# Batch 0's squares and the embeddings later at the start, transfers booked at 400 GB/s, and first turned tiles asked earlier in the second mixture

## The chip, the cores and the metric

The kernel runs on one core of one Trainium2 chip. The metric is device microseconds (us) of one execution. The engines are TensorE (PE; its weight loads are PEld), VectorE (DVE), ScalarE (ACT), GpSimd (POOL) and SyncE (SP), which here issues almost all transfers.

## The reference

Three layers follow each other. The sizes are x (8, 8, 512, 64), state (8, 8, 32, 64), 4608 tokens of 512 numbers, 2048 hidden units, and 8 experts with 1024 hidden units each.

```python
scores = scale * x @ state.T;  a = exp(scores - max);  a /= a.sum + 1e-9
xread = a @ state                                  # every x row reads the state
a2 = softmax(scale * state @ x.T) ; sread = a2 @ x # every state row reads x
tok = concat([xread, sread], axis=2) -> (4608, 512)
h = tok @ w_in ; r = max(h, 0) ; y = (r * r) @ w_out             # 512 -> 2048 -> 512
logits = unit(y) @ unit(expert_emb).T / tau ; e = argmax(logits)
gate = softmax(logits)[e]
out = gate * (max(y @ w1[e], 0) @ w2[e])                         # 512 -> 1024 -> 512
```

## The kernel before

All work is put in order by a greedy planner, the class `Plan`, when the program is built. Each piece of work is a generator, a thread with a priority, that yields an engine with an estimated cost (`yield act(1260)`), an event (`yield ev("st", 0)`), or a pool of buffers. `run` picks the step that can start first by these costs, and of equal ones the smaller priority; the order in which it picks them is the order in which the instructions of each engine stand, and that order is fixed on the chip. Transfers have a booked time too:

```python
self.dma_free = max(self.dma_free, self.cur[2]) + nbytes / 350e3   # Plan.dma: bytes per us
return self.dma_free + 2.0
phl_slots.release(t + LATE)       # weights of the experts: a buffer is free LATE us after the booked store
```

The figures move nothing on the chip by themselves: they say when the planner takes a transfer to be there, and so in which order it puts the work.

Products are split into two halves of FP16 each, three matmuls for one (lines 1442 to 1444 of the first up-projection, 1527 to 1529 of its down-projection, 1840 to 1842 and 1881 of the experts'). Each part needs a scale, a power of two from the sum of squares (`pow2`), so squares are taken all through the kernel.

**The start.** SP loads state and x of batch 0 and then the 16 blocks of w_in and w_out, 1 MB each, into buffers that are used for other things later (`RAW_IN`, names such as g, stage, wo_t, he). Each block is converted by ACT and DVE (L916, L929, L931), and for w_in a bound on the columns is found: products with itself on TensorE (L962), a diagonal of that on DVE (L971), its squares on ACT (L976), sums over partitions (L985) and a maximum on DVE (L991). From two blocks' maxima comes the scale `swi` of w_in (L999 to L303). Batch 0 goes through at once (`first_attention`, `first_scores`, `first_scale`): its x is used in FP32, its attention is applied to the product of state and w_in (S, then sw, L678), and `first_scale` squares x (L623, two operations of ACT) for the scale `sx` of batch 0. `embeddings` squares and scales the experts' embeddings on DVE (the reciprocal root `rsqrt` is lines 309 to 315). It runs at once when its small loads are there.

**Batches.** Batches 1 to 7 follow in order, and the state side of batch 0, which is called batch "B" there, stands between batches 2 and 3 (`ATT`). `late_side` waits for x of batch 0 and asks for its state side, whose two exponentials are L780 (he, rt with the factor `eighth`). x lies in the buffer xx; when the late side gives it back (`xf_slots.release()`), the other layout of x can be loaded.

**The first mixture and routing.** The up-projections u (L1442) with relu and square on ACT and DVE (L1395, L1409, L1414), and the down-projections d (L1527; in FP32 at L1505 for the first tokens) run over the batches. Each tile of 128 tokens becomes a record `rec`; a DMA transpose of it (xr, L1279, asked by SP) feeds the router's matmuls t (L1289), and POOL scatters the record to DRAM (L1368).

**The second mixture.** Tokens are sorted into tiles of one expert each. For a tile, POOL gathers its records (`gather`, L1766, name rec2), SP asks for a DMA transpose, the turn (`turn`, L1786, name xes), and `fetch_weights` loads the expert's w1 and w2 where they are not there already (L1744, 2 MB each; buffers stage and xx hold w1, he and sw hold w2). All these loads and turns stand in SP's one queue in a fixed order. In `fetch`, the loads of tile 0 wait for `ev("experts")` and `ev("attention")`, those of tile 1 also for

```python
if t == 1:
    yield ev("moe1") if name == "w2" else ev("cum", NXT - 1)
    yield ev("xe", 0)          # the first turn, as booked to be done
```

Of the kernel before, what the change touches and what calls it, by code (L numbers as in the profile page):

```python
# [10 lines left out]
F32 = mybir.dt.float32  # L11
# [52 lines left out]
PRIO_E1 = 2.2  # L64
PRIO_SW = 1.27
TINY = 0.18
LATE = 3.0


C_ID = 0  # L70
# [34 lines left out]
class Plan:  # L105
# [32 lines left out]

    def dma(self, nbytes):

        self.dma_free = max(self.dma_free, self.cur[2]) + nbytes / 350e3
        return self.dma_free + 2.0

    def _advance(self, th):
# [102 lines left out]
def moe_kernel(  # L247
# [317 lines left out]
    def first_attention():  # L565

        yield ev("st", 0)
        stt = st_t.pop(0)
        yield xhl_slots
        xh, xl = halves_tile()  # L570
        ss = small.tile([128, 3], F32, name="ss")
        yield act(490)
        nc.scalar.activation(out=xl.bitcast(BF16)[:, :, :64], in_=stt, func=AF.Square, accum_out=ss[:, 2:3])
        yield t_slots
        p = ps_t.tile([128, 512], F32, name="t")
        yield "pe", 0.2
        mm(p[:, 2:3], lhsT=one32, rhs=ss[:, 2:3], start=True, stop=True)
        mm(p[:, 256:512], lhsT=oneb, rhs=xl.bitcast(BF16)[:, :, :64], start=True, stop=True)
        for t in range(2):
            plan.add(first_scores(t, xh, xl, stt), 0.4 + 0.1 * t)  # L580
        plan.add(first_scale(ss, stt), 0.95)
        v = small.tile([128, 2], F32, name="sv")[:, 0:1]
        yield tiny(4)
        V.tensor_scalar(out=v, in0=p[:, 2:3], scalar1=FLOOR, scalar2=None, op0=ALU.max)
        pow2(sx[:, 1:2], isx[:, 1:2], v, 204)
        yield sth_slots
        sthl = att.tile([128, 2, 4, 64], F16, name="sthl")
        stf = sthl.rearrange("p a c n -> p (a c n)").bitcast(F32).rearrange("p (c n) -> p c n", c=4)
        yield dve2(256)
        V.tensor_scalar(out=stf, in0=stt, scalar1=sx[:, 1:2], scalar2=float(2.0 ** -14), op0=ALU.mult, op1=ALU.mult)  # L590
        ev("stf").set()
        plan.add(first_state_w(stf), 0.6)
        plan.add(group_bound(0, p), 0.7)
# [15 lines left out]
        yield from weigher(0, Sp.rearrange("p a (h n) -> p (a h) n", n=NS), xh, xl, eighth, 16 * t, 16 * t + 16,  # L609
                           lambda: u_slots.release(k_h))  # L610

    def first_scale(ss, stt):

        for t in range(2):
            yield ev("scored", t)
        yield ev("stf")
        st_slots.release()
        xf = xf_t.pop((0, 0))
        for i in range(2):
            yield pjk_slots  # L620
            jk = att.tile([128, 2, 512], BF16, name="pjk")
            yield act(1260)
            nc.scalar.activation(out=jk, in_=xf[:, 2 * i:2 * i + 2], func=AF.Square, accum_out=ss[:, i:i + 1])  # L623
            pjk_slots.release()
        xf_slots.release()
        at = plan.now()
        yield t_slots
        plan.cur[2] = max(at, plan.now())
# [11 lines left out]
    def late_side():  # L640

        yield ev("x", B, 0)
        yield ev("st", B)
        xf, stt = xf_t.pop((B, 0)), st_t.pop(B)
        yield ev("att", ATT[ATT.index(B) - 1])
        plan.add(state_side(B, ((stt, xf),), eighth), PRIO_S0)
        for C in range(2):
            yield ev("ST", B, C)
        xf_slots.release()
        st_slots.release()  # L650

# [99 lines left out]
    def state_side(b, pairs, scl):  # L751
# [37 lines left out]
        nc.sync.dma_start_transpose(e, eb[:, 1024:2048].bitcast(F16))  # L789
        turned = plan.dma(1 << 19) + 1.0  # L790
        yield ev("x", b, 1)
        xs = xf_t.pop((b, 1))
        yield xhl_slots
        xsh, xsl = halves_tile()
# [425 lines left out]
    def embeddings():  # L1220
# [3 lines left out]
        nc.scalar.dma_start(cs16, cst16)  # L1224
        plan.cur[2] += 2.5
        ev("identb").set()
        yield tiny(3)
        V.reciprocal(out=itau, in_=tsb)
        V.tensor_scalar(out=itau, in0=itau, scalar1=float(2.0 ** -14), scalar2=None, op0=ALU.mult)
# [484 lines left out]
    def fetch_weights(t0, t1):  # L1714
        def fetch(name, done, ts, slots, src):
            last = None
            for t in ts:
# [9 lines left out]
                else:  # L1727
# [4 lines left out]
                    if t == 1:  # L1732

                        yield ev("moe1") if name == "w2" else ev("cum", NXT - 1)
                        yield ev("xe", 0)
                sides = sides_of(t)
                for i, a in enumerate(sides):
                    if i and last + 1 < t:
# [17 lines left out]
    def gather(t0, t1, m2):  # L1756
        for t in range(t0, t1):
# [1 line left out]
            yield ev("idx", which)  # L1759
            yield ev("records", (NT if which else SEEN) - 1)  # L1760
            if t == 2:
                yield ev("xe", 0)
            yield rec2_slots
            r = m2.tile([128, REC], F32, name="rec2", bufs=6)
            yield "pool", 1.1
# [14 lines left out]
    def turn(t0, t1, m2):  # L1780
        for t in range(t0, t1):
# [2 lines left out]
            xe = m2.tile([128, 8, 128], F16, name="xes", bufs=XE)  # L1784
            yield "sp", 0.06
            nc.sync.dma_start_transpose(xe, rec_t[t].bitcast(F16)[:, 0:1024])  # L1786
            plan.cur[2] = plan.dma(1 << 18) + 1.0
            xe_t[t] = xe
            ev("xe", t).set()
# [220 lines left out]
```

## Time and profile before

| | us |
|---|---|
| three runs | 1068.17, 1074.14, 1078.63 |
| their median | 1074.14 |
| the profiled execution, its own time | 1067.83 |
| span of its trace | 1066.0 |
| TensorE busy in it | 1029.7 (97%) |
| VectorE busy | 671.4 (63%) |
| ScalarE busy | 591.9 (56%) |
| GpSimd busy | 125.8 (12%) |
| moved by DMA | 212.93 MB, 200 GB/s on average |

The time of an execution holds the span and 1.8 us around it. All times of the trace count from the start of the span, in one profiled execution. The busy shares are averages over stages with different limits.

### The profile page before, as it was taken

The page shows a single profiled execution, that of the slowest core. Times are in us where ns is not written, and L with a number is a line of the kernel's source. Part 1 is how long each engine was busy: PE and PEld are TensorE (multiplying, and loading weights), DVE is VectorE, ACT ScalarE, POOL GpSimd, SP SyncE. Part 2 cuts the span into 40 slices and gives each one's busy share as a digit, 9 for nine tenths or more (in the row PEclk, how much of TensorE's full clock was granted, in tenths as well). Part 3 has the DMA queues.
Part 4 walks back from the last instruction along what each step waited for, and adds up shares of the span by engine and source line. Part 5 has one row for each costly group of instructions (what it writes and reads, how often), then busy time and mean ns, then how long its engine had stood idle before and what let it go on. Part 6 is the DMA issues. An engine that isn't in the chain of part 4 may idle for free. (4 is left out here: it accounts for less than half of the span.)

```text
span 1066.0 us, 26360 instructions
## 1 busy us (share of the span) xinstructions
PE 1029.7 (97%) x10631; PEld 670.7 (63%) x10631; DVE 671.4 (63%) x1835; ACT 591.9 (56%) x986; POOL 125.8 (12%) x149
## 2 busy tenths in 40 slices
PE   5899999999999999989999999899999999999998
PEld 4555555565655565546655667577767677767675
DVE  6899898689797888877877876356322223222222
ACT  5999987788888798777887895110111011111110
POOL 0000001002002010020020010312112121212111
PEclk9999999999999999999999999999999999999999
DMA  8943656827757568676575896954894677684692
GB/s 302 342 146 112 170 163 143 269 75 167 245 115 223 163 184 240 170 188 195 129 225 156 238 327 222 287 136 110 277 317 108 206 236 228 190 257 114 214 324 80
DMA packets 161600, 212.93 MB, mean 200 GB/s; under 512 B 112257, under 2 KB 115201, under 8 KB 156098
## 3 DMA queue, kind: packets, MB, share of 16 engines
q1 hardware_dynamic: 152722, 184.04, 59.6%
q0 software_dynamic: 8320, 27.08, 7.8%
q8 instruction: 85, 1.39, 0.5%
q14 instruction: 41, 0.34, 0.1%
q10 hardware_dynamic: 432, 0.08, 0.0%
HBM read 259.10 MB, written 51.68 MB: 292 GB/s over the span
## 5 line engine op out<-in xcount | busy, mean ns | idle before, releaser
L1796 ACT ACTIVATE r<-u 128x512 f32<-128x512 f32 x70 | 41.8, 597 | 321.4 <-PE u L1842 304.0
L1527 PE MATMUL d<-wo_t,g 128*128 128x512 f16 x512 | 194.1, 379 | 0.9 <-DVE rec L318 0.9
L1529 PE MATMUL d<-wo_t,g 128*128 128x512 f16 x512 | 194.1, 379 | 0.6 <-DVE g L1414 0.6
L1528 PE MATMUL d<-wo_t,g 128*128 128x512 f16 x512 | 194.0, 379 | 0.0
L1442 PE MATMUL u<-aT,sw 128*128 128x256 f16 x512 | 140.8, 275 | 4.0 <-ACT r L1395 3.4
L1444 PE MATMUL u<-aT,sw 128*128 128x256 f16 x512 | 140.5, 274 | 0.0
L1443 PE MATMUL u<-aT,sw 128*128 128x256 f16 x512 | 140.5, 274 | 0.0
L1799 DVE CAST hh<-r 128x512 f16<-128x512 f32 x70 | 29.9, 427 | 156.5 <-ACT r L1796 155.0
L1395 ACT ACTIVATE r<-u,cg 128x512 f32<-128x512 f32 x128 | 87.5, 684 | 55.3 <-PE u L1444 42.1
L1368 POOL DMA_INDIRECT rec_d<-rec,pi x34 | 39.5, 1163 | 471.7 <-ACT r L1409 178.0
L1414 DVE TENSOR_TENSOR g<-r,g 128x512 f16<-128x512 f32 x128 | 87.1, 687 | 4.8 <-ACT r L1409 3.4
L1529 PEld LDWEIGHTS <-g 128*128 128x128 f16 x512 | 50.1, 98 | 61.8 <-DVE g L1414 1.6
L1810 DVE TENSOR_SCALAR o<-d,rec,wo_t 128x512 f32<-128x512 f32 x35 | 28.3, 809 | 83.9 <-PE d L1881 80.9
L1528 PEld LDWEIGHTS <-g 128*128 128x128 f16 x512 | 50.1, 98 | 48.0 <-issue 1.1
L1409 ACT ACTIVATE r<-r 128x512 f32<-128x512 f32 x128 | 79.4, 627 | 1.4
L1527 PEld LDWEIGHTS <-g 128*128 128x128 f16 x512 | 50.2, 98 | 47.5 <-DVE l L1323 0.4
L1881 PEld LDWEIGHTS <-hh 128*128 128x128 f16 (+1 forms) x688 | 50.9, 102 | 43.6 <-issue 0.4
L1840 PE MATMUL u<-xes,stage 128*128 128x128 f16 x448 | 76.0, 219 | 0.8 <-DMA xes<-rec 0.8
L1842 PE MATMUL u<-xes,stage 128*128 128x128 f16 x448 | 76.0, 219 | 0.0
L1841 PE MATMUL u<-xes,stage 128*128 128x128 f16 x448 | 76.0, 219 | 0.0
L1840 PE MATMUL u<-xes,xx 128*128 128x128 f16 x416 | 71.7, 221 | 2.0 <-DMA xx<-w_d 2.0
L1842 PE MATMUL u<-xes,xx 128*128 128x128 f16 x416 | 71.7, 221 | 0.0
(337 smaller groups left out, 2562.7 us busy)
## 6 DMA issues: line engine op xcount, KB each, us to landing
w_d<-he SPq DMA_DIRECT2D x128, 256.0 KB
g<-w_d SPq DMA_DIRECT2D x16, 2048.0 KB
wo_t<-w_d SPq DMA_DIRECT2D x16, 2048.0 KB
stage<-w_d SPq DMA_DIRECT2D x14, 2048.0 KB
he<-w_d SPq DMA_DIRECT2D x14, 2048.0 KB
xx<-w_d SPq DMA_DIRECT2D x13, 2048.0 KB
sw<-w_d SPq DMA_DIRECT2D x13, 2048.0 KB
stage<-in_w_dram SPq DMA_DIRECT2D x20, 1024.0 KB
```

Of the source, the lines that this page charges most:

```text
L1395: nc.scalar.activation(out=r, in_=ps, func=AF.Relu, scale=cg[:, g:g + 1] if u >= F32U else cgq[:, c:c + 1])
L1409: nc.scalar.activation(out=r, in_=r, func=AF.Square)
L1414: V.tensor_tensor(out=gl, in0=r, in1=gh, op=ALU.subtract)
L1442: mm(o, lhsT=hl[:, i, 0, fs], rhs=aT[:, i, :], start=i == 0, stop=False)
L1443: mm(o, lhsT=hl[:, i, 0, fs], rhs=aT[:, 2 + i, :], start=False, stop=False)
L1444: mm(o, lhsT=hl[:, i, 1, fs], rhs=aT[:, i, :], start=False, stop=i == 1)
L1527: mm(ps, lhsT=g_h[:, f, ts], rhs=w[:, 0, :], start=f == 0, stop=False)
L1528: mm(ps, lhsT=g_h[:, f, ts], rhs=w[:, 1, :], start=False, stop=False)
L1529: mm(ps, lhsT=g_l[:, f, ts], rhs=w[:, 0, :], start=False, stop=f == KF - 1)
L1840: mm(p[:, j, xs], lhsT=w[:, 0, k, fs], rhs=xe[:, k, xs], start=k == 0, stop=False)
L1841: mm(p[:, j, xs], lhsT=w[:, 0, k, fs], rhs=xe[:, 4 + k, xs], start=False, stop=False)
L1842: mm(p[:, j, xs], lhsT=w[:, 1, k, fs], rhs=xe[:, k, xs], start=False, stop=k == 3)
```

## The change

In batch 0's part, the two squares of x, the sum behind them and the scale `sx` leave the start. A new thread `first_read` gives back the state's buffer and one of x's buffers when the scores are done; `first_scale` is now asked by `late_side`, squares the x that this has loaded, and sets a new event "first squares", which x's buffer waits for, while batch 0's state side waits for "first sx". `embeddings` waits for the load of block 12. In the planner transfers are booked at 400 instead of 350 bytes per ns, and `LATE` is 2 instead of 3 us. In the second mixture a new event "xe asked" says that a turn has been issued: the loads of tile 1 and the gather of tile 2 wait for it instead of for the turn's booked end, and the first w2 waits for the second turn to be issued.

```diff
--- before.py
+++ after.py
@@ -64,7 +64,7 @@
 PRIO_E1 = 2.2
 PRIO_SW = 1.27
 TINY = 0.18
-LATE = 3.0
+LATE = 2.0
 
 
 C_ID = 0
@@ -138,7 +138,7 @@
 
     def dma(self, nbytes):
 
-        self.dma_free = max(self.dma_free, self.cur[2]) + nbytes / 350e3
+        self.dma_free = max(self.dma_free, self.cur[2]) + nbytes / 400e3
         return self.dma_free + 2.0
 
     def _advance(self, th):
@@ -578,7 +578,7 @@
         mm(p[:, 256:512], lhsT=oneb, rhs=xl.bitcast(BF16)[:, :, :64], start=True, stop=True)
         for t in range(2):
             plan.add(first_scores(t, xh, xl, stt), 0.4 + 0.1 * t)
-        plan.add(first_scale(ss, stt), 0.95)
+        plan.add(first_read(), 0.95)
         v = small.tile([128, 2], F32, name="sv")[:, 0:1]
         yield tiny(4)
         V.tensor_scalar(out=v, in0=p[:, 2:3], scalar1=FLOOR, scalar2=None, op0=ALU.max)
@@ -609,20 +609,25 @@
         yield from weigher(0, Sp.rearrange("p a (h n) -> p (a h) n", n=NS), xh, xl, eighth, 16 * t, 16 * t + 16,
                            lambda: u_slots.release(k_h))
 
-    def first_scale(ss, stt):
+    def first_read():
 
         for t in range(2):
             yield ev("scored", t)
         yield ev("stf")
         st_slots.release()
-        xf = xf_t.pop((0, 0))
+        xf_t.pop((0, 0))
+        xf_slots.release()
+
+    def first_scale(xf):
+
+        ss = small.tile([128, 3], F32, name="ss")
         for i in range(2):
             yield pjk_slots
             jk = att.tile([128, 2, 512], BF16, name="pjk")
             yield act(1260)
             nc.scalar.activation(out=jk, in_=xf[:, 2 * i:2 * i + 2], func=AF.Square, accum_out=ss[:, i:i + 1])
             pjk_slots.release()
-        xf_slots.release()
+        ev("first squares").set()
         at = plan.now()
         yield t_slots
         plan.cur[2] = max(at, plan.now())
@@ -644,8 +649,10 @@
         xf, stt = xf_t.pop((B, 0)), st_t.pop(B)
         yield ev("att", ATT[ATT.index(B) - 1])
         plan.add(state_side(B, ((stt, xf),), eighth), PRIO_S0)
+        plan.add(first_scale(xf), PRIO_A1)
         for C in range(2):
             yield ev("ST", B, C)
+        yield ev("first squares")
         xf_slots.release()
         st_slots.release()
 
@@ -789,6 +796,8 @@
         nc.sync.dma_start_transpose(e, eb[:, 1024:2048].bitcast(F16))
         turned = plan.dma(1 << 19) + 1.0
         yield ev("x", b, 1)
+        if b == B:
+            yield ev("first sx")
         xs = xf_t.pop((b, 1))
         yield xhl_slots
         xsh, xsl = halves_tile()
@@ -1224,6 +1233,7 @@
         nc.scalar.dma_start(cs16, cst16)
         plan.cur[2] += 2.5
         ev("identb").set()
+        yield ev("raw", 12)
         yield tiny(3)
         V.reciprocal(out=itau, in_=tsb)
         V.tensor_scalar(out=itau, in0=itau, scalar1=float(2.0 ** -14), scalar2=None, op0=ALU.mult)
@@ -1732,7 +1742,9 @@
                     if t == 1:
 
                         yield ev("moe1") if name == "w2" else ev("cum", NXT - 1)
-                        yield ev("xe", 0)
+                        yield ev("xe asked", 0)
+                    elif t == 0 and name == "w2":
+                        yield ev("xe asked", 1)
                 sides = sides_of(t)
                 for i, a in enumerate(sides):
                     if i and last + 1 < t:
@@ -1759,7 +1771,7 @@
             yield ev("idx", which)
             yield ev("records", (NT if which else SEEN) - 1)
             if t == 2:
-                yield ev("xe", 0)
+                yield ev("xe asked", 1)
             yield rec2_slots
             r = m2.tile([128, REC], F32, name="rec2", bufs=6)
             yield "pool", 1.1
@@ -1784,6 +1796,7 @@
             xe = m2.tile([128, 8, 128], F16, name="xes", bufs=XE)
             yield "sp", 0.06
             nc.sync.dma_start_transpose(xe, rec_t[t].bitcast(F16)[:, 0:1024])
+            ev("xe asked", t).set()
             plan.cur[2] = plan.dma(1 << 18) + 1.0
             xe_t[t] = xe
             ev("xe", t).set()
```

Since the planner orders all work anew, other instructions move too, by a few places, from the start to about 640 us; no engine's amount of work in matmuls changes. Line numbers of the new program are up to 13 higher than those of before.

On DVE at the start, between the maximum over a pair of w_in's blocks (wv) and the scale from it (swi), there stands before the change the embeddings' reciprocal root (env, rst, eny):

```order
L991 TENSOR_REDUCE wv<-u 128x1
L309 TENSOR_SCALAR rst<-env 128x8
L310 TENSOR_SCALAR eny<-rst 128x8
L313 TENSOR_TENSOR rst<-eny 128x8
L314 SCALAR_TENSOR_TENSOR rst<-rst,env 128x8
L315 SCALAR_TENSOR_TENSOR eny<-rst,eny 128x8
...
L999 TENSOR_SCALAR p2m<-wv 128x2
L1001 TENSOR_SCALAR p2m<-p2m 128x2
L299 TENSOR_SCALAR p2m<-p2m 128x2
L301 TENSOR_SCALAR swi<-p2m 128x2
```

And behind it:

```order
L1000 TENSOR_REDUCE wv<-u 128x1
L541 TENSOR_TENSOR xx<-xx,sm 128x512
L1008 TENSOR_SCALAR p2m<-wv 128x2
L1010 TENSOR_SCALAR p2m<-p2m 128x2
L299 TENSOR_SCALAR p2m<-p2m 128x2
L301 TENSOR_SCALAR swi<-p2m 128x2
```

The eleven operations of the reciprocal root have left this place; one product of batch 0's attention weights (xx) stands there. In all 25 small operations of the embeddings go behind block 12.

On SP at the start of the second mixture, the loads of w1_d and w2_d and the turns stand before the change as follows (rows of register loads left out):

```order
L1744 DMA stage_126<-w1_d_66 128x8192
...
L1744 DMA he_125<-w2_d_67 128x8192
L1786 DMA_TRANSPOSE xes_9097<-rec2_9073 128x8x128
L1786 DMA_TRANSPOSE xes_9162<-rec2_9096 128x8x128
...
L1744 DMA xx_124<-w1_d_66 128x8192
L1279 DMA_TRANSPOSE xr_9219<-rec2_8805 128x8x128
...
L1744 DMA sw_127<-w2_d_67 128x8192
L1786 DMA_TRANSPOSE xes_9402<-rec2_9161 128x8x128
```

And behind it:

```order
L1756 DMA stage_126<-w1_d_66 128x8192
L1798 DMA_TRANSPOSE xes_9079<-rec2_9055 128x8x128
...
L1756 DMA xx_124<-w1_d_66 128x8192
L1798 DMA_TRANSPOSE xes_9112<-rec2_9078 128x8x128
...
L1756 DMA he_125<-w2_d_67 128x8192
L1289 DMA_TRANSPOSE xr_9236<-rec2_8806 128x8x128
...
L1756 DMA sw_127<-w2_d_67 128x8192
L1798 DMA_TRANSPOSE xes_9403<-rec2_9170 128x8x128
```

The first turn and the second w1 (xx) stand ahead of the first w2 (he) now, and the router's transpose xr stands behind that w2. On TensorE the router's matmuls on this xr stood behind the 36th matmul of the second up-projection, and stand behind the 24th of its 96 now.

On ACT in batch 0's late pass (r are the first mixture's hidden units, he with rt the pass's two exponentials), before the change:

```order
L1395 ACTIVATE r<-u,cg 128x512
L1409 ACTIVATE r<-r 128x512
L780 ACTIVATE he,rt<-t,mt,eighth 128x512
L1395 ACTIVATE r<-u,cg 128x512
L780 ACTIVATE he,rt<-t,mt,eighth 128x512
L1409 ACTIVATE r<-r 128x512
L323 ACTIVATE he<-stage,se 128x1024
```

And behind it:

```order
L323 ACTIVATE he<-wo_t,se 128x1024
L1193 ACTIVATE pjk,pacc<-stage 128x1024
L628 ACTIVATE pjk,ss<-xx 128x1024 x2
L1405 ACTIVATE r<-u,cg 128x512
L787 ACTIVATE he,rt<-t,mt,eighth 128x512
L1419 ACTIVATE r<-r 128x512
L787 ACTIVATE he,rt<-t,mt,eighth 128x512
```

The two squares of x (pjk, ss) stand right ahead of the pass's exponentials now. One more place is told in words: on TensorE the 24 matmuls of the state's product S (L704 before, L711 now) that stood behind the router's matmuls on one xr, at 477.73 us of the trace, stand ahead of them now.

## Rows read from the trace of the kernel before

**Rows 1.** The page's first part: busy time, share of the span, instructions.

```profile
PE 1029.7 (97%) x10631; PEld 670.7 (63%) x10631; DVE 671.4 (63%) x1835; ACT 591.9 (56%) x986; POOL 125.8 (12%) x149
```

**Rows 2.** TensorE's waits, whole span: for whom; us in total, times, longest.

```profile
PE t L962 <- ACT rec L916: 6.9, 2, 3.7
PE t L1289 <- DMA xr<-rec: 4.6, 3, 2.9
...
PE u L1840 <- DMA xx<-w_d: 2.0, 1, 2.0
...
PE u L1840 <- DMA xes<-rec: 0.8, 1, 0.8
```

**Rows 3.** Windows: length, busy PE, PEld, DVE, ACT, POOL, PEclk, DMA share, GB/s.

```profile
8.00:22.00 14.00, 10.58 (x73) 8.51 (x72) 11.33 (x26) 8.83 (x12) 0.00 (x0) 1.00 1.04 397
27.00:53.00 26.00, 21.74 (x189) 13.69 (x190) 23.38 (x50) 24.50 (x32) 2.40 (x5) 1.00 0.95 343
53.00:80.00 27.00, 27.00 (x219) 15.95 (x218) 25.20 (x58) 25.11 (x36) 1.38 (x3) 1.00 0.42 149
80.00:107.00 27.00, 25.55 (x186) 15.41 (x183) 25.41 (x58) 25.10 (x40) 0.00 (x0) 1.00 0.36 110
```

**Rows 4.** Windows behind the waits of rows 12 and 10, as rows 3.

```profile
479.10:482.40 3.30, 3.30 (x29) 1.88 (x14) 2.28 (x5) 1.99 (x4) 0.00 (x0) 0.50 1.08 164
690.80:694.00 3.20, 3.06 (x36) 2.80 (x34) 0.18 (x1) 0.00 (x0) 0.00 (x0) 0.50 0.94 277
```

**Rows 5.** Timeline of ACT at the start: start, length, instruction, idle before it.

```profile
12.38 1.04 ACT L623 ACTIVATE pjk<-xx 128x1024 bf16<-128x1024 f32 x1
...
21.34 1.06 ACT L976 ACTIVATE pjk<-wi 128x1024 bf16<-128x1024 f32 x1 [1.93 <-DVE wi L931]
...
28.07 0.68 ACT L678 ACTIVATE sw<-S,swi 128x512 f16<-128x512 f32 x1
```

**Rows 6.** Timeline of DVE at the start: reciprocal root and scale.

```profile
24.55 0.16 DVE L309 TENSOR_SCALAR rst<-env 128x8 int32<-128x8 int32 x1
...
26.56 0.17 DVE L315 SCALAR_TENSOR_TENSOR eny<-rst,eny 128x8 f32<-128x8 f32 x1
26.64 0.28 DVE L999 TENSOR_SCALAR p2m<-wv 128x2 f32<-128x2 f32 x1
...
27.36 0.17 DVE L301 TENSOR_SCALAR swi<-p2m 128x2 int32<-128x2 int32 x1
```

**Rows 7.** Timeline of TensorE at the start: first up- and down-projection.

```profile
32.26 0.42 PE L1442 MATMUL u<-aT,sw 128*128 128x256 f16 x1
...
39.55 7.08 PE L1505 MATMUL d<-wo_t,g 128*128 128x512 f32 x16
```

**Rows 8.** Timeline of ACT in batch 0's late pass.

```profile
191.19 0.69 ACT L1395 ACTIVATE r<-u,cg 128x512 f32<-128x512 f32 x1 [1.30 <-PE u L1444]
...
193.62 0.69 ACT L1395 ACTIVATE r<-u,cg 128x512 f32<-128x512 f32 x1 [0.32 <-PE u L1444]
```

**Rows 9.** Timeline of SP's queue at the start of the second mixture.

```profile
673.53 2.63 SPq L1786 DMA_TRANSPOSE xes<-rec  x2
678.44 0.35 SPq L1744 DMA_DIRECT2D xx<-w_d  x1
678.89 4.07 SPq L1279 DMA_TRANSPOSE xr<-rec  x1
```

**Rows 10.** Timeline of TensorE at the start of the second mixture.

```profile
689.59 0.23 PE L1840 MATMUL u<-xes,xx 128*128 128x128 f16 x1 [2.03 <-DMA xx<-w_d]
...
692.76 0.28 PE L1289 MATMUL t<-en,xr 128*128 128x16 f16 x4
```

**Rows 11.** Timeline of POOL: the gather for the second mixture's first tiles.

```profile
665.94 1.13 POOL L1766 DMA_INDIRECT rec<-rec_d,wo_t  x1 [42.92 <-PE u L1451]
```

**Rows 12.** Timeline of TensorE at one router product, and the state's product behind.

```profile
477.73 0.26 PE L1289 MATMUL t<-en,xr 128*128 128x16 f16 x4 [2.87 <-DMA xr<-rec]
...
478.69 1.16 PE L704 MATMUL S<-wi,sthl 64*32 64x512 f16 x24
```

## The prediction, made before the result

> **What bounds the kernel now.** I read the page's first part, then TensorE's waits over the whole span, then windows, then the timelines of the places that the change touches. TensorE is busy 1029.7 of 1066.0 us [rows 1]. What is left is 36 us, so a change that removes no matmul of weight can only win idle time, or time in which the clock is low. The list of waits shows where the idle time is [rows 2]: converted w_in blocks from ACT near the start (6.9 us), transposed rows xr for the router (4.6 us, one of them 2.9), and at the start of mixture 2 the first turned tile (0.8) and the second w1 (2.0). Behind the waits of 2.9 and 2.0 us the granted clock is 0.50, its 1.2 GHz level, for 3.3 and 3.2 us of the windows shown; it is 1.00 (2.4 GHz) in the other windows [rows 3, 4]. Half of such a stretch is lost, 1.6 us each, on top of the wait. The windows also show that from 27 to 107 us ACT and DVE have little room either [rows 3].
>
> **The change part by part.** The sum is made against the profiled execution, 1067.83 us, which is 6.3 below the median of the three runs, 1074.14; I put the same difference on the median.
>
> 1, the start. What leaves the road to the first scale of w_in: two squares on ACT (1.04 us each [rows 5]), five small DVE operations for batch 0's scale, and 25 small DVE operations of the embeddings. Eleven of these (the reciprocal root) stand between the last reduce that the scale needs and the scale: the first starts at 24.55, the next operation behind the last at 26.64, which is 2.1 us or 0.19 each [rows 6]. In the new order one other operation stands there. ACT's 2.1 us come off the same chain: the second block's conversion and square are behind them, and that square waited 1.93 us for DVE [rows 5]. So the scale, ready at 27.5 [rows 6], can come at most 2.1 + 2.1 = 4.2 us earlier, and with it ACT's first product with the state at 28.07 [rows 5], the first up-projection at 32.26 and the first FP32 down-projection at 39.55 [rows 7]. But the 25 operations come back behind block 12. At the same pace they are 4.8 us, and they fall into the two windows in which DVE is idle 1.80 and 1.59 us [rows 3]. If DVE sets the pace there, 4.2 - 4.8 = -0.6 is left; if all its idle time takes them in, 2.8; if ACT or TensorE set it, 4.2. I take 1.8, the middle of -0.6 and 4.2, since DVE and ACT are about equally full there.
>
> The loads land at 397 GB/s in the window from 8 to 22 us [rows 3], which is what the new booking says. A rule of the Trainium skill speaks against this booking: "DMA: Bandwidth & Descriptors", Specifications, gives about 358 GB/s of memory to each core, by which each load would be booked a tenth too short and every consumer would come too early. The trace does not agree, and by the row the sum takes no charge for it.
>
> 2, batch 0's late pass. The two squares now stand ahead of that pass's two exponentials, and x's buffer is free only behind them, so SP's load of the other layout of x waits for ACT too; behind it in SP's queue stand a state load and stores of experts' weights. ACT is idle 1.30 and 0.32 us beside this pass [rows 8], against 2.1 us of squares. Cost 0.5; bounds 0 and 2.1, the squares in full. The scale's five DVE operations and its small matmul go into idle time of the same kind, at nothing; without that cover they are 1.0 us at the pace above.
>
> 3, the start of mixture 2. SP now asks for w1 and w2 of the first tile, then two turns, then the second w1 at 678.44, on which TensorE waits until 689.59, and behind it a router transpose xr, used at 692.76 [rows 9, 10]. From asking to use the 2 MB took 11.15 us. In the new order the first turn stands ahead of the second w1 and the second turn ahead of the first w2. The first turn needs its gathered rows; POOL asks for them at 665.94, not earlier, since it waits for TensorE's last use of w_in [rows 11]. SP could ask for the turn at 673.53 [rows 9], 7.6 us later, with 2 MB of w2 in the same queue (5.3 us at 397 GB/s). Without these the rows land between 668.2 and 673.5; I take 670.5. A turn takes SP 1.3 us, and 2.3 pass from the second turn's end to the next load (676.16 to 678.44 [rows 9]). So the second w1 is asked at 674.1, is there at 685.3 by the same 11.15 us, and TensorE comes to it at 686.8 (689.59 less both waits). The waits of 0.8 and 2.0 go, and 1.6 of low clock: 4.4 us.
>
> In exchange the first w2 is asked at 678.1 (one more turn and 2.3), about where the second w1 is now, and xr stands behind it. By the same times w2 is there at 689.2, soon enough for the down-projection, which follows the whole second up-projection; xr is there 3.2 us later (692.76 less 689.59), at 692.4. TensorE wants xr 24 of 96 matmuls into that up-projection: 2.1 us at the pace of 36 matmuls between 689.59 and 692.76 [rows 10], at 688.9. So at worst a new wait of 3.5 with 1.6 of low clock behind it, at best none, if w2 takes 7 us with the gathers out of its way. Gain between 4.4 and -0.7; I take 1.8, the middle.
>
> 4, the moved order. The booked rate and the shorter allowance shift what each engine does next by a few operations between 50 and 640 us; the work is the same. One place can be read: the wait of 2.87 us for xr at 477.73 [rows 12]. In the new order 24 more matmuls of a state product, 1.16 us in the row behind it [rows 12], stand ahead of that router matmul. If the transpose lands when it did, 1.7 us of wait are left: a gain of 1.2, or 2.8 with the clock. Elsewhere the same shift can open such a wait as well as close one. I take -1.2; bounds -4.5 (2.87 and 1.6 gone) and +4.5 (one like it new).
>
> Sum: -1.8 + 0.5 - 1.8 - 1.2 = -4.3 us: 1063.5 for a profiled execution, 1069.8 on the median.
>
> **Rivals.** A, all gains at once: the start keeps 4.2, mixture 2 keeps 4.4, and the wait at 477.73 goes with its clock, 4.5. That is -13.1, 1061.0. For it: the three lie in different stretches, and TensorE is the bound between them. Against: DVE's windows [rows 3], and xr behind w2.
>
> B, the queue at the start of mixture 2 turns against the change, and the kernel is slower. While SP waits for the first rows, the queue can stand empty, and the 2 MB that were moved then come 5.3 us later in all; behind them stand xr, the second w2 and the third turn. Price: 5.3 of waits, spread over xr and the third turn, with twice 1.6 for the clock, less the 4.4 won: +4.1. With the start's gain at 0, part 2 at 0.5 and part 4 at -1.2 that is +3.4, 1077.5. It decides when w2, asked at 678.1, lands behind 685.7 (688.9 less 3.2). For it: the router transpose behind the second w1 took SP 4.07 us to ask [rows 9], so the queue was full. Against: the second w1 and the gathers are gone by then. The Trainium skill, on the same page, Queues, rings and completion order, says that a DMA engine takes a ring's descriptors in order. By that rule xr cannot pass w2; the trace agrees as far as xr was used 3.2 us behind w1.
>
> C, real loads in the middle come later than booked: those that share the queue with stores and scatters meet TensorE's fixed order too late. Two more waits like the one at 477.73, 4.5 each, with parts 1 to 3 as forecast: -3.1 + 9.0 = +5.9, 1080.0. For it: that wait happened [rows 12]. Against: of three waits on xr it is the only one of its size [rows 2].
>
> D, the change does not do what it says: the scale is early, but DVE gives it back by 107 us, and mixture 2 waits as long as now on another transfer. Then part 2's 0.5 is left: 1074.6.
>
> **How the numbers follow.** Chances: forecast 0.50 (its own range 1064 to 1074, parts 1 and 3 between their better halves and nothing), A 0.20, B 0.12, C 0.06, D 0.12. The range, 1060 to 1078, takes in A, the forecast, D and most of B; C and the edges of A and B are left out. One per cent of 1074 is 10.7 us, about what a measurement of this kernel can tell from no change (its three runs span 10.5). Faster by more than that, under 1063.4: A and a small part of the forecast, 0.22. Slower, over 1084.9: only B and C together, 0.04. Within: 0.74.
>
> **What would show it.** Part 1: the first up-projection near 28 to 29 us instead of 32.26, the FP32 down-projection near 35, and DVE still full from 53 to 107. Part 2: the squares beside batch 0's late exponentials, and no new gap of TensorE over 1 us there. Part 3: no wait on the first turn or the second w1, and a wait on xr, w2 or the third turn in their place, with a low clock if it is 2 us or more. Part 4: one or two waits on xr at other places. The prediction is wrong if TensorE's idle time in the span stays at 36 us or more, or falls under 25.

## The result

The changed kernel is slower by about 1%: 1084.68 us (median of 4, 1082.13 to 1089.76) against 1072.85 for before, ratio 1.0116, interval 1.008 to 1.0151. Measured twice more it gave 1.0093 (1.0067 to 1.012) and 1.0086 (1.0052 to 1.0119). The forecast was 1069.8 with a range up to 1078, so it had the wrong sign and the measured time lies outside the range.

The profiled execution took 1085.56 us, its span is 1083.8. The page's first part:

```profile
PE 1036.0 (96%) x10631; PEld 671.6 (62%) x10631; DVE 676.7 (62%) x1851; ACT 581.0 (54%) x970; POOL 120.5 (11%) x149
```

TensorE has as many matmuls as before and is busy 6.3 us longer [rows 1]. About 2.5 us of that are the low clock (half of what it is busy in the low stretches below, 11.4 us, less the 6.4 of before [rows 4]); the rest is spread over its matmuls and is not taken apart here. Its idle time rose from 36.3 to 47.8 us; the prediction had named 36 or more as a sign of being wrong. TensorE's waits over the span (us in total, times, longest):

```profile
PE u L1452 <- ACT r L1405: 12.8, 9, 3.4
PE u L1853 <- DMA xes<-rec: 4.9, 2, 4.6
...
PE t L1299 <- DMA xr<-rec: 3.2, 1, 3.2
PE t L971 <- ACT rec L925: 2.8, 2, 2.3
```

The w_in waits of the start (L971) fell from 6.9 to 2.8, and the router's from 4.6 to 3.2 [rows 2]. New are 4.6 us on the second turned tile (L1853) and 9.4 us more of waits behind ACT in the first mixture (12.8 in all, 3.4 before). Windows, columns as in rows 3:

```profile
53.00:80.00 27.00, 26.94 (x181) 14.90 (x179) 25.18 (x71) 22.06 (x30) 1.99 (x3) 1.00 0.39 144
80.00:107.00 27.00, 22.72 (x200) 15.51 (x199) 25.42 (x68) 23.95 (x41) 0.00 (x0) 1.00 0.35 105
257.00:263.80 6.80, 5.82 (x20) 2.90 (x20) 5.19 (x7) 6.55 (x11) 0.37 (x2) 0.50 0.79 180
697.30:707.40 10.10, 5.60 (x58) 5.37 (x59) 0.18 (x1) 0.00 (x0) 0.00 (x0) 0.50 0.99 386
```

TensorE is idle 4.3 us from 80 to 107 (1.45 before [rows 3]), and two stretches of 6.8 and 10.1 us run at clock 0.50, its 1.2 GHz level; before there were two of about 3.3 [rows 4] (the first 35 and the last 4 us of the span left out). The start of the second mixture, first SP's queue, then TensorE:

```profile
665.18 0.37 SPq L1756 DMA_DIRECT2D stage<-w_d  x1
676.49 1.26 SPq L1798 DMA_TRANSPOSE xes<-rec  x1
680.32 0.36 SPq L1756 DMA_DIRECT2D xx<-w_d  x1
680.78 3.93 SPq L1798 DMA_TRANSPOSE xes<-rec  x1
687.24 0.06 SPq L1756 DMA_DIRECT2D he<-w_d  x1
687.93 9.95 SPq L1289 DMA_TRANSPOSE xr<-rec  x1
```

```profile
698.63 0.26 PE L1853 MATMUL u<-xes,xx 128*128 128x128 f16 x1 [4.57 <-DMA xes<-rec]
...
704.51 0.27 PE L1299 MATMUL t<-en,xr 128*128 128x16 f16 x4 [3.17 <-DMA xr<-rec]
```

The first gather is asked at 672.87, the first turn 3.6 us behind it and the second w1 7.5 us behind it; before it was 7.6 and 12.5 us [rows 9, 11]. But the second turn stands behind the 2 MB of the second w1 now. Asked at 680.78, it is used at 698.63, 17.9 us later. POOL's queue meanwhile (rec_d<-rec is a scatter, rec<-rec_d a gather):

```profile
682.26 1.02 POOL L1378 DMA_INDIRECT rec_d<-rec,pi  x1 [2.92 <-DVE rec L1374]
683.59 1.03 POOL L1778 DMA_INDIRECT rec<-rec_d,wo_t  x1 [0.31 <-issue]
684.92 1.03 POOL L1378 DMA_INDIRECT rec_d<-rec,pi  x1 [0.30 <-issue]
```

Two more scatters follow at 686.25 and 687.56. Before, both turns were asked from 673.53 on and the first scatter at 675.33, behind them.

### The profile page after: what moved, and what is told of

Same layout as the page of the kernel before. It is cut to its first block, busy times and chain, and to the rows that moved or that the text cites. A ratio compares the mean times of both kernels' runs of the same rounds, so it can differ in the third digit from the quotient of the medians.

```text
span 1083.8 us, 26370 instructions
## 1 busy us (share of the span) xinstructions
PE 1036.0 (96%) x10631; PEld 671.6 (62%) x10631; DVE 676.7 (62%) x1851; ACT 581.0 (54%) x970; POOL 120.5 (11%) x149
## 5 line engine op out<-in xcount | busy, mean ns | idle before, releaser
L1452 PE MATMUL u<-aT,sw 128*128 128x256 f16 x512 | 141.3, 276 | 13.6 <-ACT r L1405 12.8
L1378 POOL DMA_INDIRECT rec_d<-rec,pi x34 | 35.5, 1043 | 502.1 <-DVE is L303 138.0
L1537 PEld LDWEIGHTS <-g 128*128 128x128 f16 x512 | 50.6, 99 | 48.3 <-issue 1.8
L1853 PE MATMUL u<-xes,xx 128*128 128x128 f16 x416 | 72.8, 223 | 4.6 <-DMA xes<-rec 4.6
L1853 PE MATMUL u<-xes,stage 128*128 128x128 f16 x448 | 76.2, 219 | 0.4 <-DMA xes<-rec 0.4
L1854 PE MATMUL u<-xes,xx 128*128 128x128 f16 x416 | 72.8, 223 | 0.5 <-issue 0.4
```

Source lines behind the costliest of these rows:

```text
L1452: mm(o, lhsT=hl[:, i, 0, fs], rhs=aT[:, i, :], start=i == 0, stop=False)
L1537: mm(ps, lhsT=g_h[:, f, ts], rhs=w[:, 0, :], start=f == 0, stop=False)
L1853: mm(p[:, j, xs], lhsT=w[:, 0, k, fs], rhs=xe[:, k, xs], start=k == 0, stop=False)
L1854: mm(p[:, j, xs], lhsT=w[:, 0, k, fs], rhs=xe[:, 4 + k, xs], start=False, stop=False)
```

## The experiments

Ratios are to the kernel before on the same chip, with 95% intervals. "Mixture 2" means the change's three edits there, "start" the squares and the embeddings, "booking" the two numbers. TensorE's waits are those of one profiled execution of each run.

**The parts.** Each alone on the kernel before, and start with booking:

> The kernel before with the second mixture's part of the change alone (the event "xe asked" and the three waits on it). Up to 650 us its order is that of before. Theory 1, the new queue order costs: the second turn stands behind the 2 MB of the second w1 and the router's transpose xr behind the first w2, so TensorE waits some 4.5 us on the second turned tile and some 3 us on xr, with 10 us of low clock instead of 3.4: +8 us, 1.007 to 1.008 of before. Theory 2, the loss comes from the order moved by the booked rate and at the start: this run is the same as before or 1 to 4 us faster, and TensorE has no wait over 2 us between 640 and 720 us.

> The kernel before with the booking alone (400 instead of 350 bytes per ns, LATE 2 instead of 3). Theory 1: the moved order opens some waits and closes others, within 2 us of before, ratio 0.998 to 1.002. Theory 2: the order is made for transfers that come later than booked, so TensorE gets new waits of 2 to 4 us on transposes (aT or xr) between 250 and 640 us with a low clock behind them: +4 to +8 us, 1.004 to 1.008.

> The kernel before with the start alone (batch 0's squares and scale in the late pass, the embeddings behind block 12), at the old booking. Theory 1: the first up-projection comes 5 to 7 us earlier, and it is given back by 130 us, since VectorE and ScalarE are full from 30 to 107 us: 0 to -2 us, ratio 0.998 to 1.000. Theory 2: the moved order opens new waits behind 130 us here too: +2 to +5 us.

> The changed kernel without the second mixture's part, so the start and the booking together with the old queue order there. Theory 1: 8 us faster than the changed kernel and 2 to 5 us slower than before (1.002 to 1.005). Theory 2: as slow as the changed kernel, 1.010 to 1.013.

```diff
 e1:  -yield ev("xe", 0)   +yield ev("xe asked", 0)   (and first w2, gather)
 e2:  -nbytes / 350e3  LATE = 3.0   +nbytes / 400e3  LATE = 2.0
 e3:  +plan.add(first_read(), 0.95) ... +yield ev("raw", 12)
 e4:  the changed kernel without the edits of e1
```

Mixture 2 alone: 1.0043 (1.0017 to 1.0069). Booking alone: 1.0118 (1.0079 to 1.0157). Start alone: 1.0006 (0.998 to 1.0032). Start and booking: 1.0021 (0.9995 to 1.0046). So the parts do not add: the booking's 12 us go when the start changes too. The profile of e1 has TensorE wait 5.6 us on the second turned tile and 1.4 on xr. Theory 1 holds for mixture 2 in its waits, not in its size (8 us forecast, 4.6 measured); theory 2 is right of the booking only where it stands alone.

**Inside mixture 2.** On one chip, the changed kernel again and three variants:

> The changed kernel itself, on the same chip as the next three. Theory 1, the queue at the start of the second mixture: 1.009 to 1.013 of before again, with waits of 4 to 6 us on the second turned tile and of 1 to 3 us on xr there. Theory 2, a good part of the loss lies in waits behind 130 us that came by chance in the first profile (3.45 us at 258, 2.75 us at 559): those do not come back, and the ratio falls to 1.004 to 1.007.

> The changed kernel with one pair exchanged in SP's queue: the loads of tile 1 wait for the first turn's booked end as before, so the second turn stands ahead of the second w1 again; the first w2 stays behind both. Theory 1, the turn behind 2 MB is the cost: the wait on the second turned tile goes, at most 1 to 2 us on the second w1 stand in its place, xr still waits 1 to 3 us behind the first w2: 5 to 8 us faster than the changed kernel, 1.003 to 1.006 of before. Theory 3, the queue that stands empty until the first rows land is the cost: the 2 MB are late all the same, and TensorE waits as long on the second w1: within 2 us of the changed kernel.

> The changed kernel with the other half taken back: the first w2 is asked right behind the first w1, as before, and only the second w1 stands ahead of the second turn. Theory 1: the wait on the second turned tile stays at 4 to 6 us, the one on xr falls under 1 us: 2 to 4 us faster than the changed kernel, 1.006 to 1.010 of before. Theory 3, the empty queue: with the 2 MB of w2 moved in that time the loss goes, within 2 us of before plus 0.2 per cent, 1.001 to 1.004.

> The changed kernel at the old booking (350 bytes per ns, LATE 3): start and second mixture alone. Theory 1: the start's 1.0006 with the cost of the second mixture's order, 4 to 10 us: 1.005 to 1.010. Theory 4, booking and start belong together, since the booking alone cost 12 us and the two together nothing: taking the booking away would leave it at 1.005 or lower, and the second mixture's cost then hangs on the booking.

```diff
 e6:  t == 1:                 -yield ev("xe asked", 0)   +yield ev("xe", 0)
 e7:  t == 0 and name == "w2":  -yield ev("xe asked", 1)
 e8:  -nbytes / 400e3  LATE = 2.0   +nbytes / 350e3  LATE = 3.0
```

The changed kernel again: 1.0093. Second turn ahead of the second w1 (e6): 1.0036 (1.0018 to 1.0054), 7.0 us less by the medians, no wait on a turned tile above 0.9 us, and 4.1 us on xr. First w2 early (e7): 1.0071 (1.0047 to 1.0095). No booking (e8): 1.0052 (1.0031 to 1.0072), which is start alone plus 0.46%, about what mixture 2 costs on the kernel before; it is also 5.1 us less than the changed kernel by the medians, so there the booking is worth about as much as mixture 2, and theory 4 is neither shown nor ruled out. The place of the second turn is the larger part of mixture 2's loss; how much of the 7.0 us it is stays open, since e5's profile also has a wait near 258 us (below) that e6's has not. The queue that stands empty is not the cost (theory 3 falls): in e7 the first w2 fills it, and TensorE waits 3.6 us on the first turned tile, whose gathered rows land beside that load, and 2.6 on xr. The wait on the second turned tile, forecast to stay at 4 to 6 us, is not in e7: the turn lands at 692.9, and TensorE comes to that tile at 698.8, behind xr's matmuls. For with an edit here the planner moves TensorE's order in this stretch too (some 100 matmuls against the changed kernel in e6 and in e7), and each ratio is that of the edit with its order.

**One exchange, and the two numbers apart:**

> The kernel before with one edit of the second mixture: the loads of tile 1 wait until the first turn is asked, not until it is booked to be done. In SP's queue this exchanges the second turn and the second w1, and nothing else up to there; the first w2 stays where it was. Theory 1, the turn behind 2 MB is the cost: the second turn lands some 5 us after the second w1, TensorE waits 3 to 5 us for it with a low clock behind: +2 to +5 us, 1.002 to 1.005 of before. Rival, the cost lies in the first w2 and the router's transpose behind it: the same as before, 0.999 to 1.001.

> The kernel before with transfers booked at 400 bytes per ns and LATE as before. If the booked rate is what cost 12 us in the run with both numbers, 1.008 to 1.014 of before; if it was LATE, within 2 us, 0.998 to 1.002.

> The kernel before with LATE 2 instead of 3 and the old rate. The rival to the run before: 1.008 to 1.014 if the stores' buffers are given back too early in the plan, so that SP's queue fills with waiting stores; within 2 us otherwise.

> The kernel before with batch 0's squares and scale in the late pass alone; the embeddings stay at the start. By the prediction's part 1, 2.1 us less on the road to the first scale and 0.5 more in the late pass: -1 to -2 us, 0.998 to 0.999. If VectorE and ScalarE give back whatever the start wins by 94 us, or the squares hold up the late pass: 0 to +3 us, 1.000 to 1.003.

```diff
 e9:   t == 1: -yield ev("xe", 0)   +yield ev("xe asked", 0)     (first w2 and gather as before)
 e10:  -nbytes / 350e3   +nbytes / 400e3
 e11:  -LATE = 3.0       +LATE = 2.0
 e12:  e3 without  +yield ev("raw", 12)
```

The one exchange of e9 costs 1.0046 (1.0023 to 1.0069), all that e1 does. Its wait is not on the second turned tile, as was expected, but on xr, which stands behind the turn (6.3 us there; the other three are at other places); TensorE's waits in e9:

```profile
PE t L1289 <- DMA xr<-rec: 10.7, 4, 6.3
```

The rate alone: 1.0184 (1.0158 to 1.021). LATE alone: 1.0153 (1.0126 to 1.0179). Each costs more alone than both together, and with the start both cost next to nothing (e4 against e3), but 5.1 us with start and mixture 2 (e5 against e8). So neither number is right or wrong by itself; each deals the order anew. Where e11's loss lies can be read in TensorE's waits, SP's queue and POOL:

```profile
PE u L1840 <- DMA xes<-rec: 9.4, 1, 9.4
```

```profile
658.88 12.09 SPq L340 DMA_DIRECT2D w_d<-he  x8
672.99 0.36 SPq L1744 DMA_DIRECT2D stage<-w_d  x1
675.08 0.34 SPq L1744 DMA_DIRECT2D he<-w_d  x1
680.67 2.40 SPq L1279 DMA_TRANSPOSE xr<-rec  x1
683.17 12.01 SPq L1786 DMA_TRANSPOSE xes<-rec  x2
```

```profile
677.27 1.03 POOL L1368 DMA_INDIRECT rec_d<-rec,pi  x1 [1.98 <-DVE gt L838]
...
681.25 0.98 POOL L1368 DMA_INDIRECT rec_d<-rec,pi  x1 [0.30 <-issue]
```

Here the deal put four scatters, and xr, ahead of the turns, and TensorE waits 9.4 us on the first turned tile; the low clock in and behind that wait lasts 10.2 us. SP is late already ahead of that: eight stores of weights (w_d<-he) hold it from 658.88 on, and the first w1 is asked at 672.99, 0.15 us behind the first gather, where before it was asked 7.6 us ahead of it (658.39 [rows 11]). That fits the queue of waiting stores that the expectation named; no run tested it. e2 shows the same, with a wait of 10.3 us. e10 has none there, but waits of 2.2 to 5.1 us at 100, 226 and 269 us, each with 3.4 us of low clock, and two under 2 us near 685 with 6.8. Its new waits end with work of ACT and DVE, not with a transfer, and e11 loses 1.5% at the old rate; that speaks against loads that come later than booked as the whole cause, though no run separates the two. Squares alone: 0.9996 (0.9973 to 1.0018), no difference.

**What holds up the turn:**

> The changed kernel with one wait more: the first of POOL's four scatters at the start of the second mixture waits for the second turn to be done; all instructions and their order are those of the changed kernel. Theory S, the scatters hold up the turn: the second turn lands within 2 us of the second w1 ahead of it, some 8 to 10 us after that is asked, the wait on the second turned tile falls under 2 us, and xr lands later, since the scatters now meet it: 1 to 5 us faster than the changed kernel (1.005 to 1.009 of before) if xr is not held up as long. Theory M, the 2 MB alone: the turn lands 15 us or more after it is asked, and the kernel is as slow as the changed one or slower, since the scatters come later, 1.009 to 1.013.

> The changed kernel with both suspects taken out of the way: the second turn ahead of the second w1, and the router's transpose xr ahead of the first w2 (which waits for that transpose to be asked). If turn and xr are the whole cost of the second mixture's order, no wait over 1.5 us between 670 and 715 us and 1.000 to 1.002 of before, 2 us or more below the run with the second turn ahead alone. If the empty queue or the first w2 costs too, it stays at 1.003 or more.

> The kernel before with the first w2 behind two turns, second w1 and xr. If the transition is the last thing that waits there, its waits of 0.8 and 2.0 us and the low clock go: -2 to -4 us, 0.996 to 0.998 of before. If the scatters or the later w2 take their place: 1.000 to 1.003.

> The kernel before with the embeddings behind block 12 alone, the squares at the start. By the prediction's part 1, 2.1 us less on the road to the first scale, given back at 4.8 us of VectorE: between -2 and +3 us. If the start never sets the end, since VectorE and ScalarE are full up to 107 us: 0.999 to 1.002. A number above 1.006 would be the moved order, as with the booking.

```diff
 e13:  +if i0 == 28:   # the four scatters' group, which is also planned behind the second turn
       +    yield ev("xe asked", 1)
       ...
       +    tc.add_manual_dep(put, turned[1].name, Sync, reason="turn")
 e14:  e6, and t == 0 and name == "w2":  -yield ev("xe asked", 1)   +yield ev("xr asked", 32)
 e15:  before, with  +elif t == 0 and name == "w2": yield ev("xr asked", 32)
 e16:  before, with  +yield ev("raw", 12)  in embeddings
```

e13 has one wait more than the changed kernel, every instruction in the same order, and a lower ratio, 1.0057 (1.0035 to 1.0079) against 1.0086 to 1.0116; its interval overlaps two of these three, and no run of the changed kernel stands on that chip, so by time alone it is not shown to be faster. The profile shows which wait went. SP's queue, POOL and TensorE in e13:

```profile
677.36 0.36 SPq L1762 DMA_DIRECT2D xx<-w_d  x1
677.82 4.11 SPq L1804 DMA_TRANSPOSE xes<-rec  x1
684.01 0.34 SPq L1762 DMA_DIRECT2D he<-w_d  x1
684.45 3.40 SPq L1290 DMA_TRANSPOSE xr<-rec  x1
```

```profile
690.01 1.22 POOL L1381 DMA_INDIRECT rec_d<-rec,pi  x1 [13.58 <-ACT rec L323]
```

```profile
691.02 0.22 PE L1859 MATMUL u<-xes,xx 128*128 128x128 f16 x1
...
694.98 0.27 PE L1300 MATMUL t<-en,xr 128*128 128x16 f16 x4 [2.46 <-DMA xr<-rec]
```

The scatters start at 690.01 (the row puts their idle time down to ACT; in this kernel they also wait for the turn), and the turn is done by then (its semaphore rises at 689.2, 11.4 us after it was asked and 2.6 behind the second w1's). In the changed kernel the semaphores rise at 691.7 (w1) and 698.5 (turn), 6.8 apart and 17.7 after the turn was asked. TensorE begins the second tile at 691.02 without a wait, and 2.46 us on xr are left. So both matter: the turn comes behind the 2 MB, and of its 17.7 us 6.3 go when the scatters are held back. The gather between them in POOL's queue (683.59 above) is held back with them, so what it takes and what they take is not told apart. Theory S holds in kind (it had forecast 8 to 10 us and less than 2 behind w1), M alone does not.

e14: 1.0082 (1.0054 to 1.0111), where at most 1.002 was forecast if turn and xr were the whole cost. xr ahead of the first w2 still made TensorE wait 4.3 us for it: it was asked at 681.30 and the scatters came from 681.43, ahead of the first w2 (686.73), so it is not w2 that holds xr up. (This execution also had the wait near 258 us, below.) e15: 1.0024 (1.0 to 1.0048); the waits on the second w1 went, and 1.9 us on xr and 1.8 on the first w2 took their place. e16: 1.0098 (1.0067 to 1.013), with new waits of 1.5 to 3.0 us at 72, 75, 129 and 415 us: the moved order again, since with the squares (e3) it costs nothing.

**On one chip:**

> The changed kernel a third time, on one chip with the next. If the wait near 258 us belongs to the program, it is there again with 3 us or more and a low clock; if it belongs to the execution, it may be anything from 0.5 to 3.5 us.

> The changed kernel without the second mixture's part, again. If the queue order at the second mixture is the whole difference, 5 to 6 us below the changed kernel (0.5 per cent); if the wait near 258 us goes with it, 9 to 11 us below, with a wait under 1 us there.

The changed kernel took 1074.62 us, without mixture 2 1068.87, before 1064.25 (1.0086 and 1.0026). So 5.75 of the 10.4 us are mixture 2, and 4.6 are start and booking (2.8 by the ratio, and 2.2 in e4). TensorE's waits in e17, then in e18:

```profile
PE u L1853 <- DMA xes<-rec: 4.5, 2, 4.0
PE t L1299 <- DMA xr<-rec: 4.2, 2, 3.6
```

```profile
PE u L1850 <- DMA xes<-rec: 3.5, 1, 3.5
```

With the old queue order e18 waits 3.5 us on the first turned tile (e4 3.4), where e17 waits 0.5 and then 4.0 on the second and 3.6 on xr: the first turn's half of the edit works, and the two transfers behind it take more than it wins. The 4.6 us can be read in the waits of L1452 behind ACT, 8.3 to 8.4 us in e4, e17 and e18 and 3.4 before, but no run takes them apart.

The wait near 258 us was 0.49 in both. Of the nine profiles of this order four have it at 3.3 to 3.5 us with 3.4 to 6.8 us of low clock (the first of the changed kernel, e5, e13, e14), and five at 1.9 or less. One program, the changed kernel, has it in two profiles and not in the third, so it belongs to the execution; with half of the low clock it is worth some 4.5 to 6.5 us in an execution that has it. It does not show between the measurements: e5 and e17 lose the same by the medians, 10.3 and 10.4 us, and one of their profiles has it and one has not. ACT and TensorE at this place in the changed kernel:

```profile
257.25 0.69 ACT L1405 ACTIVATE r<-u,cg 128x512 f32<-128x512 f32 x1 [2.60 <-remote]
```

```profile
257.99 0.37 PE L1452 MATMUL u<-aT,sw 128*128 128x256 f16 x1 [3.45 <-ACT r L1405]
```

TensorE waits for ACT, and ACT for TensorE: the semaphore that tells it that a block of u is done rises at 257.22 for a last matmul that ends at 253.23 by the trace, and at 257.35 for one that ends at 254.54; in e17, where the wait is 0.49, it rises 0.02 us behind both ends. In all four profiles with the wait the second rise comes 2.6 to 2.8 us late. So TensorE's results, or their semaphore, come later than the trace ends those matmuls. What causes it stays open.

## Why the prediction was wrong

**Part 3, the step that failed.** It said that the waits of 0.8 and 2.0 us go and that in exchange at worst 3.5 come on xr: -1.8, bounds -4.4 and +0.7. Measured: +4.6 (e1, by ratio), +4.9 (e8 against e3, by ratio) and +5.75 us (e17 against e18, by medians). Its times up to there were right: the second w1 was forecast to be asked at 674.1, and it was asked at 680.32 less the 6.93 by which this execution ran late (672.87 against 665.94 at the first gather), 673.4. The waits of 0.8 and 2.0 went (0.3 on the first turned tile, none on w1), and xr's new wait, 3.17 us, lay in its bound of 3.5. The prediction followed every transfer but one: the second turn, which the edit put behind the 2 MB of the second w1, got no arrival time, and so the wait on it was put at nothing; it is 4.57 us, with the low clock beside it. The two fences of SP's order showed the exchange. With the 11.15 us that it used for a load in this queue the w1 is there at 685.3, and with the 3.2 us that it used for xr behind a load the turn at 688.5, 1.7 us after TensorE wants it: a wait in place of the 2.0 won. And the turn took 6.8 us behind w1, not 3.2; the scatters that POOL asks at that moment were in the trace and in no term.

The Trainium skill, "DMA: Bandwidth & Descriptors", Queues, rings and completion order, says that a DMA engine serves the queues that have work in turn, a packet from each, and one ring's descriptors in order. The runs agree: the turn keeps its place behind the w1 of its own queue, and three of POOL's scatters and its gather, asked later on another queue, pass it (they land from 693.8 to 697.7, the turn at 698.5).

**Rival B** had the side, the place and nearly the price: +4.1 us there, at a chance of 0.12. Its mechanism was half right: behind the first w1, asked at 665.18, the queue has one turn to move until 680.32, but e7 showed that filling it does not help. The first w2 landed far behind its point of decision (703.6, which is 696.7 by the old clock, against 685.7), but TensorE waits as long for xr when no w2 stands ahead of it (4.3 us in e14). **Rival D** had both mechanisms, a start given back and a wait on another transfer, but priced that wait at no more than the old ones.

**Part 1** was right in what it could see. The scale from w_in, forecast at most 4.2 us earlier, comes at 23.50 instead of 27.36; DVE, then TensorE:

```profile
23.50 0.17 DVE L301 TENSOR_SCALAR swi<-p2m 128x2 int32<-128x2 int32 x1
```

```profile
25.18 0.39 PE L1452 MATMUL u<-aT,sw 128*128 128x256 f16 x1
...
34.18 0.42 PE L1454 MATMUL u<-aT,sw 128*128 128x256 f16 x1
34.39 1.78 PE L1515 MATMUL d<-wo_t,g 128*128 128x512 f32 x3
```

The first up-projection is 7.1 and the FP32 down-projection 5.2 us earlier [rows 7]. All of it is given back. Windows of before and then of the changed kernel, columns as in rows 3:

```profile
0.00:36.00 36.00, 19.83 (x136) 15.45 (x138) 26.22 (x72) 23.32 (x31) 0.77 (x9) 1.00 0.92 316
36.00:130.00 94.00, 91.28 (x782) 52.51 (x767) 86.39 (x194) 87.81 (x132) 3.78 (x8) 1.00 0.55 174
```

```profile
0.00:36.00 36.00, 21.70 (x119) 14.46 (x120) 23.00 (x50) 23.14 (x30) 0.77 (x9) 1.00 0.91 307
36.00:130.00 94.00, 88.63 (x749) 50.59 (x748) 86.76 (x207) 83.34 (x125) 3.06 (x8) 1.00 0.55 177
```

By 36 us TensorE has been busy longer, but with 119 matmuls of all sizes instead of 136. The prediction read a clock of 1.00 in the windows of rows 3; at the start that is no measurement, since the trace's record of the clock begins at 35.3 us before and 35.0 us in the changed kernel. Ahead of that, matmuls of 256 columns start 0.21 us apart, as in the stretch at 0.50 near 258 us, and behind it 0.11. TensorE before:

```profile
35.03 0.42 PE L1444 MATMUL u<-aT,sw 128*128 128x256 f16 x1
...
35.52 0.27 PE L1444 MATMUL u<-aT,sw 128*128 128x256 f16 x1
```

So the up-projections that came earlier ran at half the pace, which the forecast had not counted. Behind 36 us it is as the prediction feared: DVE is busy 50.6 of the 54 us from 53 to 107, as before. e3, the start alone, is at 1.0006 (0.998 to 1.0032). The forecast kept 1.8 us; the value to take was nothing, which lay in its bounds. **Part 2** held: the squares stand at 189.68 and 190.86 on ACT, right ahead of the exponentials, and TensorE waits 1.4 us at 189.7 where it waited 1.0 at 188.7. By itself the move is worth nothing (e12, 0.9996).

**Part 4** is the other step that failed. It saw its one place rightly, the 2.87 us at 477.73 are gone (1.5 us of other gaps stand there), and was wrong to price a moved order by one place. Bounds of 4.5 us either way were far too narrow: moving the order by a number alone cost 12 to 20 us (e2, e10, e11) and by the embeddings' place 10 (e16). Parts 1, 2 and 4 together were forecast at -2.5 and measured at +2 to +5 (e4, e18). On the chip of e17 and e18 the forecast of -4.3 met +10.4; some 7.5 of this miss are part 3 and 7.1 the other parts. That the loads land at 397 GB/s was taken as a reason to charge nothing for the booking; but the booking acts through the order, not through the transfers.

The chance of 0.04 for slower by over 1% was too low: of the three measurements one is over 1% and two are just under it.

## What to carry to other kernels

When loads are reordered in a queue, give every transfer of that queue an arrival time, the small ones behind the large above all: a transpose of 256 KB behind 2 MB waited here for these and for what another queue asked meanwhile. A change to the numbers of a greedy planner is a new deal of the whole order, worth what its new waits cost with the low clock beside them; it has to be measured together with all else that changes, since its parts do not add. Work that was taken off the way to the first matmul won nothing here: the matmuls that came earlier ran at the lower clock, and the stage behind was full on the engine that the work moved to.

## What was not expected of the hardware

A wait added on GpSimd took a wait of TensorE away: four scatters and a gather, held back some 10 us, let the turn land 2.6 instead of 6.8 us behind the load ahead of it (e13). Asking for a DMA transpose took SP 1.25 us when the queue was short and 3.1 to 11 us behind a load (9.95 for the xr above, 11.0 in e1), and all that stands behind it in the queue is asked that much later. The length of a wait alone does not tell whether the low clock follows: 2.03 us before [rows 4, 10] had 3.2 us of it, and 2.75 us at 559 us in the changed kernel and 2.56 us at 331 us in e3 had none. And one order of instructions gave, near 258 us, a wait of 0.5 us in some executions and of 3.4 with up to 6.8 us of low clock in others, in which TensorE's semaphore rose 2.6 to 2.8 us late.
